# Splitting the early output weights into eight-partition DMAs in a DMA-bound decode kernel

## The chip, the cores and the metric

One core of one Trainium2 chip. The metric is the device time of one execution in microseconds (us); medians of several executions are quoted. One kernel's times agree within about 0.1 to 0.2% unless the text says otherwise.

## The reference

Eight sequences each decode one token: a layer norm with modulation, attention over a cache of 8192 keys and values with 8 key/value heads and 32 query heads, the output projection with `wo`, then a small MLP. Cut to what matters:

```python
# B = 8, D = 512, Hq = 32, Hkv = 8, Sk = 8192, Dh = 128, all bf16
h = layernorm(x) * (1 + ca) + sa
q = (h @ wq)                                   # 8 x 32 heads x 128
scores = einsum('bhqd,bhkd->bhqk', q, k_cache) * Dh ** -0.5
p = softmax(scores)
o = einsum('bhqk,bhkd->bhqd', p, v_cache)
x = x + ga * (o.reshape(B, 1, Hq * Dh) @ wo)   # wo: 4096 x 512
...                                            # layer norm, modulation
x = x + gb * (relu(h @ w1 + b1) ** 2 @ w2 + b2)
```

The two caches are 268 MB of the 284 MB that the kernel moves. `wo` is 4 MB.

## The kernel before

The caches come as 64 units of 4 MB, 128 rows (SBUF partitions) by 32 KB, through a ring of four slots. SyncE (SP) issues all of these DMAs in order on one queue. A unit's slot is loaded again as soon as TensorE has read it.

```python
units = [(kv, b, p) for b in range(B) for kv in "kv" for p in range(NP)]   # NP = 4
...
def load(n):
    kv, b, p = units[n]
    s = n % NSLOT
    src = ...                                    # 128 partitions x 32 KB
    dep = [released.get(s)]
    if units[n] == last:
        ...                                      # the last V unit, in four pieces
    else:
        loaded[n] = dma("sync", s_ring[s], lambda e: e.dma_start(slot(s), src), dep)
...
load(0)
load(1)
d_b1 = ...; d_b2 = ...                           # two small rows
wo_e = wo_sb[:, 0:24, :].rearrange("p (g j) n -> p g (j n)", j=4)
d_woe = dma("sync", s_woe, lambda e: e.dma_start(       # the early output weights, 3 MB
    wo_e, A_wo[0:24 * DH, :].rearrange("(g p j) n -> p g (j n)", g=6, p=128)))
d_wo = dma("sync", s_wo, lambda e: e.dma_start(         # the late output weights, 1 MB in 1 KB runs
    wo_sb[:, 24:32, :], A_wo[24 * DH:, :].rearrange("(h dh) n -> dh h n", dh=DH)))
load(2)
load(3)
```

TensorE transposes each K unit, computes scores with it, later multiplies the V units, and at the end runs the output projection and the MLP. The end needs, in this order, the last two V units, then W1 and W2, which lie in ring slots and are loaded last. The early output weights are used only at the end, so it doesn't matter when they land; what matters is whose time they take.

## Time and profile before

The kernel took 680.5 us (680.34 to 680.65).

| what | before | where it is read |
|---|---|---|
| span of the profiled execution | 677.9 us | the page |
| DMA share, rate in the middle | above 90%, 430 GB/s | the page's slices |
| TensorE busy | 73% | the page |
| K unit 2 (the first loaded behind the output weights) lands | 59.86 to 61.64 us | completion semaphores in the trace |
| unit due at 634 us lands | 623.20 to 627.32 us on eight engines, 632.46 to 634.31 us on the other eight | the same |
| last V piece lands | 652.5 to 656.7 us on eight, 661.9 to 663.74 us on eight | the same |
| last W2 piece lands | 664.3 to 665.7 us on eight, 672.2 to 673.95 us on eight | the same |

How to read it: in the trace the completion semaphore of every DMA of 128 rows climbs in 16 steps, one from each DMA engine when its own part has landed, and so these steps show how far apart the engines are. "Lands on eight at ..." means eight of these steps.

From the page of the kernel before: the span, the DMA lines of the slices (40 equal slices; busy share in tenths, then GB/s), the instruction queue (packets, MB, share of the 16 engines' span), and the chain that ended last, by engine.

```profile
span 677.9 us, 15869 instructions
...
DMA  8999999999999999999999999999999999999994
GB/s 365 439 400 434 430 431 433 430 431 425 424 433 429 428 431 433 432 430 431 432 433 425 418 432 430 429 427 431 431 433 432 430 424 426 431 429 431 427 393 160
...
q8 instruction: 57, 0.93, 0.6%
...
PE 49%; DMA 45%; DVE 3%; ACT 2%; issue 1%; SPq 0%
```

The DMA engines are the bound: they are above 90% from the second slice to the last but one. The chain is TensorE for half of it, because each batch has a stretch in which TensorE works on units that have already landed; but each such stretch begins when a landing lets it. Queue 8 is the engines' own instruction fetch: 57 packets of 16 KB (the Trainium skill, "Runtime: NRT & Kernel Launch", "Instruction fetch mechanics", gives blocks of 16 KiB, 256 instructions; 57 packets carry 0.93 MB here, which agrees). Each takes about 1.07 us. The trace doesn't name the engine of a packet. That they go in turn to only eight of the 16 DMA engines is read from the landings: eight engines fall behind, one of them at each fetch. Seven fetches of 1.07 us are 7.5 us, most of the distance between the two groups in the table, but not all: after 48 fetches, six for each of the eight, the medians of the two groups are already 9.3 us apart (the unit that lands from 584.4 to 594.0 us), or about 1.5 us for each fetch. The engines that fall behind keep the lag from unit to unit, and the kernel ends with them.

The chain of waits of the kernel before at both ends of the run, in order of time (start us, us, what).

```profile
23.18 38.46 DMA ring<-in_A_k_cache_dram
61.64 0.05 issue
61.69 3.60 PE PS L344 x32
```

```profile
569.44 24.57 DMA ring<-in_A_k_cache_dram
594.06 6.41 PE PS L344 x64
...
648.68 25.27 DMA ring<-in_B_w_dram
674.00 0.82 PE PS L569 x24
```

TensorE starts K unit 2 when it lands (61.69 us), starts the last batch when its first K unit lands (594.06 us), and waits once more for W2 (674.00 us). The waits of the kernel before after 600 us (engine, line, what it waited for: us in total, times, longest) show how little slack there is at the end:

```profile
PE PS L438 <- DMA ring<-in_A_v_cache_dram: 0.9, 1, 0.9
...
PE PS L569 <- DMA ring<-in_B_w_dram: 0.2, 1, 0.2
```

Two short waits: anything that delays the latest engine by more than a microsecond delays the end by nearly as much, and anything that makes it earlier gains about one microsecond.

The last view is SP's own timeline in the kernel before: start, duration, line, operation. Where a DMA instruction is long, many packets were still waiting in front of it: that of K unit 2 ended at 44.91 us.

```profile
3.46 0.40 SPq L323 DMA_DIRECT2D wo_sb<-in_A_wo_dram  x1
3.90 19.24 SPq L325 DMA_DIRECT2D wo_sb<-in_A_wo_dram  x1
23.18 22.60 SPq L261 DMA_DIRECT2D ring<-in_A_k_cache_dram  x2
```

### The profile page before, as it was taken

The numbers are of one execution on the slowest core, as the hardware profiler recorded it, in microseconds if no ns is written. First come the engines' busy times: TensorE is split into PE (matmuls) and PEld (weight loads), VectorE is DVE, ScalarE is ACT, GpSimd is POOL, SyncE is SP. The second block draws the span as 40 slices with busy tenths as digits, with TensorE's granted clock in tenths as the row PEclk, the third lists the DMA queues.
The fourth block names the chain that finished last, engine by engine and source line by source line (L and its number), as shares of the span: only waits on it lengthen the run. The fifth ranks groups of instructions, "written<-read, shape, count | busy, mean of one in ns | idle before, by whom it ended". The sixth has DMA issues, their size and how long they took to land.

```text
span 677.9 us, 15869 instructions
## 1 busy us (share of the span) xinstructions
PE 496.7 (73%) x7372; PEld 352.5 (52%) x7372; DVE 298.4 (44%) x558; ACT 234.9 (35%) x280; POOL 16.7 (2%) x66
## 2 busy tenths in 40 slices
PE   2394964997649965698548975499656987399777
PEld 2383731775237741576317752387325763187535
DVE  2062731567116751367215661167513673156712
ACT  2052620465006630265204650056302652046600
POOL 7200000000000000000000000000000000000000
PEclk9996985899769977799868987599766997589975
DMA  8999999999999999999999999999999999999994
GB/s 365 439 400 434 430 431 433 430 431 425 424 433 429 428 431 433 432 430 431 432 433 425 418 432 430 429 427 431 431 433 432 430 424 426 431 429 431 427 393 160
DMA packets 13733, 284.67 MB, mean 420 GB/s; under 512 B 1218, under 2 KB 2275, under 8 KB 4708
## 3 DMA queue, kind: packets, MB, share of 16 engines
q1 hardware_dynamic: 13620, 283.65, 98.0%
q8 instruction: 57, 0.93, 0.6%
q14 instruction: 8, 0.07, 0.0%
q10 hardware_dynamic: 48, 0.02, 0.0%
HBM read 283.66 MB, written 0.01 MB: 418 GB/s over the span
## 4 chain that ended last, share of the span: by engine, by line
PE 49%; DMA 45%; DVE 3%; ACT 2%; issue 1%; SPq 0%
DMA ring<-in_A_k_cache_dram 37%; PE PS L344 33%; PE PS L359 8%; DMA ring<-in_A_v_cache_dram 4%; DMA ring<-in_B_w_dram 4%; PE PS L438 3%; PE PS L401 3%; ACT KTb L349 1%; ACT P_sb L392 1%; DVE m L364 1%; PE PS L419 1%; DVE Pm L414 0%; DVE rinv L420 0%; DVE rhs_r L417 0%; DVE Dm L385 0%
## 5 line engine op out<-in xcount | busy, mean ns | idle before, releaser
L349 ACT ACTIVATE KTb<-PS 128x1024 bf16<-128x1024 bf16 x192 | 196.5, 1024 | 378.3 <-PE PS L344 378.3
L344 PE MATMUL PS<-IDENT,ring 128*128 128x128 bf16 x4096 | 269.6, 229 | 46.3 <-DMA ring<-in_A_k_cache_dram 46.2
L344 PEld LDWEIGHTS PS<-IDENT,ring 128*128 128x128 bf16 x4096 | 248.9, 103 | 95.1 <-DMA ring<-in_A_k_cache_dram 48.8
L351 DVE COPY KTb<-PS 128x1024 bf16<-128x1024 bf16 x320 | 210.2, 687 | 149.7 <-PE PS L344 147.6
L438 PE MATMUL PS<-ring,Pm 128*32 128x512 bf16 x992 | 87.7, 516 | 50.2 <-DMA ring<-in_A_v_cache_dram 45.9
L359 PE MATMUL PS<-KTb,QTm 128*32 128x512 bf16 x1024 | 79.2, 386 | 4.5 <-ACT KTb L349 4.5
L447 DVE CAST O_sb<-PS 128x512 bf16<-128x512 f32 x31 | 21.4, 692 | 130.4 <-PE PS L438 130.4
L438 PEld LDWEIGHTS PS<-ring,Pm 128*32 128x32 bf16 x992 | 30.8, 120 | 88.3 <-DMA ring<-in_A_v_cache_dram 47.1
L450 PE MATMUL PS<-SEL,O_sb 128*128 128x8 bf16 x124 | 22.5, 181 | 30.4 <-DVE O_sb L447 24.8
L450 PEld LDWEIGHTS PS<-SEL,O_sb 128*128 128x128 bf16 x124 | 12.0, 97 | 59.4 <-DVE O_sb L447 45.9
L401 PE MATMUL PS<-IDENT,P_sb 128*64 128x128 bf16 x512 | 26.1, 278 | 10.3 <-ACT P_sb L392 10.0
L401 PEld LDWEIGHTS PS<-IDENT,P_sb 128*64 128x64 bf16 x512 | 22.2, 146 | 13.0 <-ACT P_sb L392 12.6
L392 ACT ACTIVATE P_sb<-PS,negm 128x512 bf16<-128x512 f32 x32 | 21.5, 685 | 18.9 <-DVE negm L389 18.9
L414 DVE COPY Pm<-PS 64x512 bf16<-64x512 bf16 x48 | 20.2, 421 | 16.8 <-PE PS L401 15.8
L359 PEld LDWEIGHTS PS<-KTb,QTm 128*32 128x32 bf16 x1024 | 15.5, 94 | 21.1 <-ACT KTb L349 8.5
L364 DVE TENSOR_REDUCE m<-PS 128x1 f32<-128x512 f32 x32 | 22.0, 689 | 6.6 <-PE PS L359 6.6
L453 DVE TENSOR_TENSOR oTn<-PS,rinv 128x8 bf16<-128x8 f32 x31 | 6.0, 194 | 31.1 <-PE PS L450 31.1
L411 ACT ACTIVATE Pm<-PS 64x512 bf16<-64x512 bf16 x16 | 9.5, 592 | 6.4 <-PE PS L401 6.4
L304 PE MATMUL PS<-haT,ring 128*128 128x8 bf16 x128 | 3.6, 168 | 8.2 <-DMA ring<-in_A_wq_dram 8.2
L419 PE MATMUL PS<-rhs_r,ONES 128*128 128x32 f32 x16 | 4.4, 365 | 6.8 <-DVE rhs_r L417 6.8
L549 ACT ACTIVATE std<-PS,epst 128x8 f32<-128x8 f32 x1 | 0.3, 267 | 26.0 <-PE PS L547 26.0
L387 PE MATMUL PS<-Dm,R 128*128 128x4 bf16 x8 | 1.4, 178 | 10.1 <-DVE Dm L385 10.1
(110 smaller groups left out, 94.9 us busy)
## 6 DMA issues: line engine op xcount, KB each, us to landing
ring<-in_A_k_cache_dram SPq DMA_DIRECT2D x32, 4096.0 KB, 34.8
ring<-in_A_v_cache_dram SPq DMA_DIRECT2D x31, 4096.0 KB, 29.2
ring<-in_A_wq_dram SPq DMA_DIRECT2D x1, 4096.0 KB, 20.5
ring<-in_w_mod_dram SPq DMA_DIRECT2D x1, 3072.0 KB, 9.8
wo_sb<-in_A_wo_dram SPq DMA_DIRECT2D x1, 3072.0 KB, 45.5
ring<-in_A_v_cache_dram SPq DMA_DIRECT2D x1, 2048.0 KB, 24.0
ring<-in_B_w_dram SPq DMA_DIRECT2D x1, 1792.0 KB, 20.4
wo_sb<-in_A_wo_dram SPq DMA_DIRECT2D x1, 1024.0 KB, 48.0
```

The source lines that it names most:

```text
L344: t = op("tensor", lambda e, j=j, i=i: e.matmul(STG[j][:, i, :], src[:, 32 * k + 8 * j + i, :], IDENT[:, :], is_transpose=True), [loaded[n ...
L349: stg_free[j] = op("scalar", lambda e, j=j, dst=dst: e.activation(dst, STG[j], ACT.Copy), [t])
L351: stg_free[j] = op("vector", lambda e, j=j, dst=dst: e.tensor_copy(dst, STG[j]), [t])
L359: t = op("tensor", lambda e, hf=hf, q=q, rhs=rhs: e.matmul(PS[32 * q:32 * (q + 1), k, :], QTm[:, b, 2 * p + hf, :], rhs, start=(p == 0 and ...
L364: return op("vector", lambda e: e.tensor_reduce(m4[:, k:k + 1], bank(k), AX.X, ALU.max), [t])
L392: exps.append(op("scalar", lambda e, k=k: e.activation(P_sb[:, k, :], bank(k), ACT.Exp, bias=negm[:, 0:1], scale=inv_sqrt, accum_out=rs4[: ...
L401: t = op("tensor", lambda e, k=k, i=i, hf=hf, src=src: e.matmul(STG[k][64 * hf:64 * (hf + 1), i, :], src, IDENT[:, :], is_transpose=True, ...
L414: done.append(op("vector", lambda e, dst=dst, frm=frm: e.tensor_copy(dst, frm), [t, k_pm]))
L419: t = op("tensor", lambda e: e.matmul(tot_ps, ONES[:, :], rhs_r[:]), [t])
L438: t = op("tensor", lambda e, p=p, m=m, cg=cg, vt=vt, Obank=Obank: e.matmul(Obank[32 * cg:32 * (cg + 1), :], lhs[:, p, 32 * m:32 * m + 32], ...
L447: t = op("vector", lambda e, osb=osb, Obank=Obank: e.tensor_copy(osb, Obank), [t])
L450: t = op("tensor", lambda e, i=i, osb=osb, oT_ps=oT_ps: e.matmul(oT_ps, osb[:, i * 128:(i + 1) * 128], SEL[:, i, :], start=(i == 0), stop= ...
```

## The change

The early output weights are 128 rows of six 4 KB packets, 48 packets on each engine. The change splits them into twelve DMAs, of which ten have eight rows, one has 16 and one 32. The intent: a DMA of eight rows uses only the first eight DMA engines. So these carry 78 of the packets each, and the other eight carry 18. At some 0.16 us for a packet (0.159 to 0.164 in the trace), 30 packets, 4.9 us of work, move from one half of the engines to the other. If the half that gets less is the half that runs late, the end comes sooner.

```diff
+        wo_er = A_wo[0:24 * DH, :].rearrange("(g p j) n -> p g (j n)", g=6, p=128)
+
+        def wo_part(sl):
+            return dma("sync", s_woe, lambda e: e.dma_start(wo_e[sl], wo_er[sl]))
+
+        for r in range(3):
+            for blk in range(4 if r < 2 else 2):
+                wo_part(slice(32 * blk + r, 32 * blk + r + 29, 4))
+        wo_part(slice(64 + 2, 64 + 2 + 61, 4))
+        d_woe = wo_part(slice(3, 128, 4))
-        d_woe = dma("sync", s_woe, lambda e: e.dma_start(
-            wo_e, A_wo[0:24 * DH, :].rearrange("(g p j) n -> p g (j n)", g=6, p=128)))
```

The slices with stride 4 are chosen so that a piece on partitions 0 to 63 writes one row through each of eight SBUF ports. The Trainium skill, "DMA: Bandwidth & Descriptors", "The descriptor swizzle", says which engine writes which partitions in a 128-row DMA: engines 0 to 7 write partitions 0 to 63, and engines 8 to 15 write 64 to 127. By that map the pieces on partitions 64 to 127 make the first eight engines write through ports that the other eight otherwise have to themselves. From here on, "lower" means the first eight engines, "upper" the other eight, "own-port pieces" those on partitions 0 to 63, and "other-port pieces" those on 64 to 127.

SP's list of DMAs grows by eleven; no other engine's instructions change their order.

## The prediction

> **What bounds the kernel.** The DMA engines. In the windows from 100 to 600 us the DMA share is 1.00 at about 430 GB/s; TensorE is busy 73%. The chain of waits is 45% DMA, 49% TensorE: each batch's TensorE work starts when its first K unit lands (594.06 us for the last).
>
> The 16 DMA engines don't finish together. Completion semaphores in the trace: all 16 parts of K unit 1 land within 1.80 us (by 41.27 us); the unit due at 634 us lands at 623.20 to 627.32 us on eight engines, at 632.46 to 634.31 on eight; the last W2 piece at 664.3 to 665.7 and 672.2 to 673.95. The difference is instruction traffic: 57 packets of 16 KB on the instruction queue, about 1.07 us each, in turn over eight engines: 7 x 1.07 = 7.5 us each. Followed packet by packet, the first three fetches (16.1, 28.2, 43.0 us) fell on engines that carried nothing of the eight-row loads of c and x. The Trainium skill, "DMA: Bandwidth & Descriptors", "Why a DMA increments its semaphore by 16 and not by 1": a DMA of 8 rows uses the lowest-numbered eight engines. So I take the late ones to be the upper eight.
>
> **What the change does.** The same 768 packets of 4 KB (0.16 us each): before 48 per engine, after 78 on each lower, 18 on each upper. 30 x 0.16 = 4.9 us moves from the late to the early half. Eleven more issues on SP (0.2 to 0.5 us each) cost nothing.
>
> **What it could give.** Both halves would end near 669 us. The last V units would land up to 2.4 us earlier, but TensorE's end chain waits only 0.9 us for V (653.78) and 0.2 us for W2 (674.0): 1 to 2 us.
>
> **Why I doubt it.** DMAs are issued in order, and a full queue on one engine stops the issue to all. Before shows it: the issue of the late output weights lasts 19.2 us, that of K unit 2 21.7 us (to 44.91, with some 80 descriptors per engine outstanding); the last W2 piece is issued at 660.6 us although the early engines had run dry at 659.3. After, the lower queues hold 78 packets, then 65 entries of late weights. K unit 2 gets through when about 80 remain there, an estimate of 49 to 50 us; the upper engines, starved from 42 us, start K unit 2 then, against 49.8 before. The 4.9 us become idle time, except that three engines make up one fetch.
>
> Besides, pieces on partitions 64 to 127 and stride-4 pieces share SBUF write ports ("SBUF — State Buffer", "Door 1: The DMA port swizzle"); no trace of before shows such sharing. Estimate: 0 to 3 us longer on the lower engines, holding the upper too.
>
> **Predicted:** 680.8 us, range 678.4 to 684.0; faster by over 2% 0.01, within 2% 0.98, slower by over 2% 0.01.
>
> **Right if:** DMA share dips between 42 and 50 us; the issue of K unit 2 ends at 48 us or later; it lands on the upper engines no earlier than 59.9 us, on the lower at 64 to 68; TensorE starts it after 64 us (61.69 before); the last W2 piece lands within 3 us of 673.95.
>
> **Wrong if:** issue isn't held by the full lower queues (upper landings 4 to 5 us earlier, time 678 to 679), or the late engines are the lower eight (683 to 686).

## The result, and the profile after

688.02 us (687.79 to 688.87, four executions), against 680.45 (680.34 to 680.65, four) before. The ratio is 1.0113, with a 95% interval of 1.0096 to 1.0131. Ratios here are the mean time of one kernel's fast runs over that of the other's of the same rounds, so they are not quite the ratios of the medians quoted beside them. The change is slower by 7.6 us, which is within the 2% band, but far outside the predicted range of 678.4 to 684.0. The profiled execution was the slowest of the four (688.87), so the differences between the two traces come out about 1 us larger than 7.6.

From the page of the kernel after, the same lines (its instruction queue has one packet more, 58):

```profile
span 686.8 us, 15880 instructions
...
DMA  8999999999999999999999999999999999999992
GB/s 368 441 284 403 434 427 430 427 428 431 428 436 430 427 427 430 432 426 431 428 432 427 430 431 428 433 428 429 428 428 430 428 432 430 436 426 428 426 375 107
...
q8 instruction: 58, 0.95, 0.6%
...
PE 52%; DMA 42%; DVE 4%; ACT 2%; issue 1%; SPq 0%
```

The loss is visible in a single slice: the third (34 to 51 us), where the output weights are loaded, moved 284 GB/s instead of 400, though the engines were just as busy by the record. Busy engines that move less have slower packets. That stretch in windows, first before, then after (from:to, length, the busy time of each compute engine, TensorE clock, then the two columns to look at: DMA share and GB/s):

```profile
core 0: us, PE busy (x) PEld busy (x) DVE busy (x) ACT busy (x) POOL busy (x), PEclk, DMA share, GB/s
39.00:42.00 3.00, 3.00 (x54) 2.47 (x52) 2.10 (x4) 1.81 (x2) 0.00 (x0) 1.00 0.94 380
42.00:45.00 3.00, 3.00 (x54) 2.37 (x55) 2.09 (x4) 2.16 (x3) 0.00 (x0) 1.00 1.02 406
45.00:48.00 3.00, 3.00 (x50) 2.05 (x46) 2.13 (x4) 1.71 (x3) 0.00 (x0) 1.00 1.03 392
48.00:51.00 3.00, 3.00 (x53) 2.47 (x52) 1.98 (x3) 1.51 (x3) 0.00 (x0) 1.00 1.16 407
```

```profile
39.00:42.00 3.00, 3.00 (x55) 2.37 (x56) 2.12 (x4) 1.78 (x2) 0.00 (x0) 1.00 0.91 291
42.00:45.00 3.00, 3.00 (x50) 2.05 (x50) 2.10 (x4) 2.05 (x2) 0.00 (x0) 1.00 1.00 218
45.00:48.00 3.00, 3.00 (x55) 2.47 (x52) 1.64 (x3) 2.05 (x2) 0.00 (x0) 1.00 1.08 284
48.00:51.00 3.00, 3.00 (x54) 2.47 (x51) 2.05 (x4) 1.54 (x2) 0.00 (x0) 1.00 0.78 185
```

Packet by packet, the trace of after shows two different things in these windows:

- Packets of the own-port pieces take 0.159 to 0.164 us, as before. Those of the other-port pieces take 0.30 to 0.32 us between 42 and 45 us, when upper engines work too (on what they have of the output weights), and 0.28 to 0.30 us between 47 and 50 us. The upper engines pay too: their 1 KB packets of the late output weights take 0.08 to 0.10 us beside them, 0.047 to 0.051 before.
- From 48 to 51 us the DMA share falls to 0.78: from about 49.5 us upper engines have nothing to do, because K unit 2 hasn't been issued to them yet. From 50 to 52 us only about 8.2 packets are under way at a time.

SP's timeline in the kernel after:

```profile
3.56 35.19 SPq L327 DMA_DIRECT2D wo_sb<-in_A_wo_dram  x12
38.79 1.02 SPq L334 DMA_DIRECT2D wo_sb<-in_A_wo_dram  x1
39.87 13.09 SPq L261 DMA_DIRECT2D ring<-in_A_k_cache_dram  x2
```

The x2 on the last line are K units 2 and 3; the issue of unit 2 alone lasts from 39.87 to 52.14 us. So upper engines start K unit 2 at 52.85 to 53.0 us, about 3 us later than before (49.6 to 50.1 on most engines), although they have 30 packets fewer in front of it.

| lands (us) | before | after |
|---|---|---|
| K unit 2, upper eight | 59.9 to 61.6 (all 16) | 63.58 to 64.52 |
| K unit 2, lower eight | | 68.09 to 70.28 |
| last V piece, the two latest engines | 663.63, 663.74 | 670.96, 672.21 |
| last V piece, the other late engines | 661.9 to 663.5 | 665.6 to 667.1 |
| last W2 piece, the two latest engines | up to 673.95 | 679.81, 681.03 |

The sum: lower engines land K unit 2 about 8.1 us later. That is 4.9 us for 30 more packets and 3.2 us more for slow ones (the 24 packets of the four other-port pieces at about 0.30 us in place of 0.16 make some 3.3 us). Upper engines land it about 3.5 us later, in place of 4.9 us sooner. By the times above, as an estimate, slow packets took about 4.5 us of this gain (the engines run dry at 49.5 us, and finished at 49.9 before), waiting for the issue took 3.4 us, and a slow first packet of K unit 2 took 0.8 us (2.07 us, 1.28 before). From there on the engines stream without a pause, and the shift stays to the end. The chain of the kernel after, in order of time, at the same two places:

```profile
39.87 30.41 DMA ring<-in_A_k_cache_dram
70.28 0.05 issue
70.33 3.23 PE PS L353 x32
```

```profile
575.05 27.37 DMA ring<-in_A_k_cache_dram
602.42 0.05 issue
602.47 5.17 PE PS L353 x64
...
632.06 30.23 DMA ring<-in_A_v_cache_dram
662.34 3.63 PE PS L447 x32
```

TensorE starts K unit 2 8.6 us later (70.33 against 61.69), the last batch 8.4 us later (602.47 against 594.06), and the last V unit but one 8.6 us later (662.34 against 653.78). Of the waits of the kernel after, past 600 us, that for V grew from 0.9 to 3.1 us. The 4.4 us for K is not new: it is the start of the last batch, which in the kernel before ended a wait as long at 594.06 us, outside this window.

```profile
PE PS L353 <- DMA ring<-in_A_k_cache_dram: 5.1, 2, 4.4
...
PE PS L447 <- DMA ring<-in_A_v_cache_dram: 3.1, 1, 3.1
```

### The profile page after: what moved, and what is told of

Same layout as the page of the kernel before. It is cut to its first block, busy times and chain, and to the rows that moved or that the text cites. A ratio compares the mean times of both kernels' runs of the same rounds, so it can differ in the third digit from the quotient of the medians.

```text
span 686.8 us, 15880 instructions
## 1 busy us (share of the span) xinstructions
PE 495.5 (72%) x7372; PEld 349.8 (51%) x7372; DVE 298.2 (43%) x558; ACT 235.0 (34%) x280; POOL 16.8 (2%) x66
## 4 chain that ended last, share of the span: by engine, by line
PE 52%; DMA 42%; DVE 4%; ACT 2%; issue 1%; SPq 0%
DMA ring<-in_A_k_cache_dram 37%; PE PS L353 33%; PE PS L368 8%; DMA ring<-in_A_v_cache_dram 4%; PE PS L447 4%; PE PS L410 3%; ACT KTb L358 1%; ACT P_sb L401 1%; DVE Pm L423 1%; DVE m L373 1%; PE PS L428 1%; PE PS L517 0%; PE PS L501 0%; DVE rinv L429 0%; PE PS L459 0%
## 5 line engine op out<-in xcount | busy, mean ns | idle before, releaser
L353 PE MATMUL PS<-IDENT,ring 128*128 128x128 bf16 x4096 | 266.8, 227 | 56.4 <-DMA ring<-in_A_k_cache_dram 56.4
L353 PEld LDWEIGHTS PS<-IDENT,ring 128*128 128x128 bf16 x4096 | 246.3, 102 | 104.9 <-DMA ring<-in_A_k_cache_dram 60.3
L447 PE MATMUL PS<-ring,Pm 128*32 128x512 bf16 x992 | 90.4, 529 | 50.3 <-DMA ring<-in_A_v_cache_dram 46.0
L447 PEld LDWEIGHTS PS<-ring,Pm 128*32 128x32 bf16 x992 | 31.1, 122 | 89.7 <-DMA ring<-in_A_v_cache_dram 47.1
L462 DVE TENSOR_TENSOR oTn<-PS,rinv 128x8 bf16<-128x8 f32 x31 | 6.0, 194 | 31.1 <-PE PS L459 31.1
```

Of the source, the lines that this page charges most:

```text
L353: t = op("tensor", lambda e, j=j, i=i: e.matmul(STG[j][:, i, :], src[:, 32 * k + 8 * j + i, :], IDENT[:, :], is_transpose=True), [loaded[n ...
L447: t = op("tensor", lambda e, p=p, m=m, cg=cg, vt=vt, Obank=Obank: e.matmul(Obank[32 * cg:32 * (cg + 1), :], lhs[:, p, 32 * m:32 * m + 32], ...
```

## The experiments

The theory after reading the result had two parts. **Who**: the late engines aren't just the upper eight; the change put work on an engine that was already the latest. **How**: writing partitions that belong to other engines' ports makes packets slow, on the writer and on those whose ports they are. Rivals: (A) the late engines are all of the lower eight, so the change moved work the wrong way for all; (B) eleven more DMAs cost something by themselves; (C) the stopped issue is the larger part (SP can't hand out K unit 2 to any engine while the queues of the lower ones are full); (D) the place in the queue is at fault, and pieces spread over the run would cost little. Fourteen kernels ran, some beside each other on the same chip. The expectations use the letters C and D a little differently, and say each time what they mean. In the short diffs "-" is the kernel that is named and "+" the experiment.

### m_before and m_after: who is late?

Tiny DMAs of 16, 8, 4, 2 and 1 rows ("markers") are issued behind the last W2 piece, the last load of all, and one of 8 rows directly behind the output weights. Each engine that takes part reports its arrival behind everything queued before on it. The Trainium skill, "DMA: Bandwidth & Descriptors", "Why a DMA increments its semaphore by 16 and not by 1", says that a DMA of k rows uses the lowest-numbered k engines. So an 8-row marker tells the lower eight apart from the rest, and a 4-row marker splits the lower eight.

```diff
+        def marker(i, rows, n):
+            return dma("sync", s_mk[i], lambda e: e.dma_start(mk_sb[0:rows, 176 * i:176 * i + n], w_mod[0:rows, 0:n]))
...
+        d_mk = [marker(5, 8, 144)]                 # behind the output weights
...
+                    d_mk += [marker(i, r, n) for i, (r, n) in enumerate(((16, 160), (8, 164), (4, 168), (2, 172), (1, 176)))]
```

> The kernel before with six tiny marker DMAs: one of 8 rows between the late output weights and K unit 2, and five of 16, 8, 4, 2 and 1 rows behind the last W2 piece. The packets of a marker of k rows show when each of the first k engines gets there. My theory (made after the result, from two late landings among the eight that got more work): the eight engines that carry instruction fetches are six of the upper eight and two of the lower eight. Then the 8-row marker at the end is reached by six engines at about 664 to 666 us and by two at about 672 to 674, and the 16-row one shows six more at 672 to 674. Rival A, late engines are the lower eight: all eight at 672 to 674. The premise of my prediction, late engines are the upper eight: all eight at 664 to 666. Time as before, 680 to 682 us.

> The changed kernel with the same markers. My theory: the middle 8-row marker is reached by the lower eight at about 57 to 60 us, so the engines whose K unit 2 lands at 63.6 to 64.5 are the upper eight, and those of 68.1 to 70.3 the lower eight; at the end the two lower engines with instruction fetches are the last of all (about 680 us), 8 to 9 us later than in the kernel before, the upper six 3 to 4 us later. Rival A: at the end all eight lower engines are last. Time about 688 us.

Measured: 680.24 and 688.25 us (one execution each, so their state is unknown; the kernel before gave 680.19 beside them, and 688.02 is the median of the kernel after), so the markers cost nothing that can be seen.

| marker at the end | in the kernel before | in the kernel after |
|---|---|---|
| 4 rows | 665.25 to 665.58, all early | 672.9 to 673.2 |
| 8 rows | six at 664.85 to 665.33, two at 671.97 and 672.13 | six at 672.5 to 673.0, two at 679.40 and 679.94, the last of all |
| 16 rows | eight at 664.54 to 665.30, eight at 671.85 to 673.76 | six more (the upper late ones) at 675.8 to 677.6 |

What follows: the eight engines with the instruction fetches are six of the upper eight and two of the lower eight. The 4-row marker is early on all, so the two are among the fifth to the eighth engine. Rival A falls, and so does the premise of the change and of the prediction. The change moved 4.9 us away from six late engines, and onto two late ones. In the kernel after the mid-run marker of 8 rows reached the lower engines at 57.65 to 59.37 us and they are the late group at K unit 2. The nesting of the results (all four early, six of eight early, eight of 16 early) agrees with the page's "lowest-numbered".

### x_extra8 and x_extra4: the bytes alone, on their own ports

The kernel before, plus one 2 KB packet on each of the first eight (or first four) engines at every unit from the fifth to the last but one, into unused memory on those engines' own ports. Over these 59 units that is about the 4.9 us of the change (at some 0.08 us a packet, half of a 4 KB one), spread out so that no queue fills.

```diff
+                if n >= 4:
+                    i = n % 8
+                    rows = slice(32 * (i % 2) + i // 2, 32 * (i % 2) + i // 2 + 29, 4)   # x_extra4: + 13
+                    idle[i] = dma("sync", s_idle[i], lambda e: e.dma_start(
+                        idle_sb[rows, :], A_wo[0:16, :].rearrange("(p j) n -> p (j n)", j=2)), [idle[i]])
```

> The kernel before, plus after each K or V load from unit 4 on a useless 8-row load of 2 KB rows (59 of them, about 0.08 us each) to rows whose ports belong to the lower eight engines anyway. So 4.8 us more work for each lower engine, without shared ports, without a full queue, and nothing taken from the upper ones. My theory (two of the lower eight are among the late engines): the last W2 piece lands about 4.8 us later, time 684 to 686. The premise of my prediction (the lower eight are early and have some 7 us of slack): within 1 us of before.

> The same useless loads with 4 rows, so that only the first four engines carry them: 4.8 us more on each of these. My theory (the markers put both late lower engines among the fifth to the eighth): within 1 us of before, as these four have 6 to 7 us of slack. Rival B (what costs is the number of DMAs, not who carries them): as slow as with 8 rows.

Measured: x_extra8 685.32 against 680.29 us (1.0074, 1.0059 to 1.0089); x_extra4 680.09 against 680.29 (0.9999, 0.9982 to 1.0016). In x_extra8 the last V piece lands on two engines at 668.85 and 668.88 us (663.6 and 663.7 before) and on the other late ones at 661.9 to 663.4, as before. So extra bytes on eight engines cost 5.0 us through two of them alone, and the same on the first four cost nothing. This is the bytes' share of the loss, and it shows that the slack at the end is below what was moved.

### x_twelve_even and x_rows32: more DMAs, but evenly spread

The early weights in twelve DMAs of 128 rows (half of a 4 KB run each), or in four DMAs of 32 rows with stride 4.

```diff
-        d_woe = dma(... wo_e, A_wo[0:24 * DH, :]...)          # x_twelve_even, from the kernel before
+        for g in range(6):
+            for h in range(2):
+                d_woe = dma("sync", s_woe, lambda e, g=g, h=h: e.dma_start(
+                    wo_e[:, g, 1024 * h:1024 * h + 1024], wo_er[:, g, 1024 * h:1024 * h + 1024]))
```
```diff
-        (the twelve pieces)                                   # x_rows32, from the kernel after
+        for r in range(4):
+            d_woe = wo_part(slice(r, 128, 4))
```

> The early output weights in twelve DMAs of 128 rows (one group of rows, half the columns each), so as many DMAs as the change has, but with equal shares of bytes on all engines. My theory (unequal shares, shared ports and stopped issue make the loss): within 1 us of before. Rival B (the number of DMAs on SP, and what each costs, makes the loss): 684 us or more.

> The same weights in four DMAs of 32 rows, stride 4, over all 128 partitions: equal bytes, and as the 32-row stage of the loading kernel ran at 0.16 us a packet, no shared ports. My theory: within 1 us of before. If the stride of 4 itself or small DMAs cost: like the 16-row pieces.

Measured: 680.57 against 680.19 us (1.0004, 0.9987 to 1.002) and 680.19 against 680.29 (1.0, 0.9985 to 1.0015). Rival B falls: twelve DMAs cost nothing that can be seen. x_rows32 also says what slow packets are not: a DMA of fewer rows with stride 4 over all partitions, which loads all ports evenly, runs at 0.159 us a packet.

### x_pairs16: the ports alone, with the engines evenly loaded

Eight DMAs of 16 rows, each within one half of the partitions. Every engine carries 48 packets, as before, but 16 engines write through eight ports at a time.

```diff
-        (the twelve pieces)                                   # from the kernel after
+        for h in range(2):
+            for r in range(4):
+                d_woe = wo_part(slice(64 * h + r, 64 * h + r + 61, 4))
```

> The early output weights in eight DMAs of 16 rows, stride 4, within one half of the partitions: equal bytes on every engine (48 packets each), but in each piece two engines write each port. My theory (shared ports cost): packets of 0.30 to 0.32 us in place of 0.16, K unit 2 lands about 7 us later on all engines, time 686 to 688. Rival C (only the unequal bytes and the stopped issue cost): within 1 us of before.

Measured: 688.32 against 680.29 us (1.012, 1.0105 to 1.0135), slightly above what was expected. Packets take 0.327 to 0.333 us, and K unit 2 lands at 67.81 to 70.06 us on all engines together. 48 x (0.33 - 0.16) = 8.2 us: port sharing costs as much as the whole change here, without any imbalance between engines.

### ports: the sharing by itself

A small kernel (97.39 us; its output is wrong, relative error 0.085) that loads pieces in stages, each waiting for the one before.

```python
stage("a128", A(0, 128))                       # 128 rows
stage("b8even", A(0, 29, 4))                   # 8 rows on the lower engines' ports
stage("c8odd", A(64, 93, 4))                   # 8 rows on the upper engines' ports, those at rest
stage("d8four", A(0, 8))                       # 8 rows on two ports
stage("e16even", A(0, 61, 4))                  # 16 rows within 0..63
stage("f16odd", A(66, 127, 4))                 # the change's 16-row piece
stage("g32", A(3, 128, 4))                     # the change's 32-row piece
stage("h64", A(0, 64))                         # 64 rows
stage("i_even_kv", ..., kvload=True)           # four own-port pieces, then a K unit
stage("j_odd_kv", ..., kvload=True)            # four other-port pieces, then a K unit
stage("k_kv", kvload=True)                     # a K unit alone
```

> The disputed cost by itself: a kernel that only loads, one stage after the other, 4 KB rows of the output weights and 32 KB rows of K; its output is wrong on purpose. If engines that write partitions of the same SBUF port share its rate: 128 rows 0.16 us a packet; 8 rows at stride 4 on partitions 0 to 28 or, alone, on 64 to 92 0.16 us; 8 rows on partitions 0 to 7 (two ports, four engines each) about 0.6 us; 16 rows at stride 4 within 64 partitions and 64 rows 0..63 about 0.30 us; four 8-row pieces of partitions 0 to 63 followed by a K unit: no stretching; four of partitions 64 to 127 followed by a K unit: 0.30 us for these and 2.1 to 2.4 us for the upper engines' 32 KB packets that run at the same time. If it is not the ports (but, say, the short DMAs themselves): the odd and the even pieces behave alike, and the 16-row piece takes 0.16 us a packet.

| stage | 4 KB packet | rate over the whole stage |
|---|---|---|
| 128 rows | 0.159 us | 366 GB/s |
| 8 rows, own ports | 0.159 us | |
| 8 rows, other ports, those engines at rest | 0.159 us | |
| 8 rows on two ports | 0.61 to 0.63 us at its end | 84 GB/s |
| 16 rows within one half (both stages) | 0.159 us for about 1.2 us, then 0.31 to 0.33 us | 167 to 178 GB/s |
| 32 rows, stride 4 | 0.159 us | |
| 64 rows | 0.319 us | 219 GB/s |

A packet is slow when its port serves two engines at once, and not when the port is merely another engine's. The Trainium skill, "SBUF — State Buffer", "Door 1: The DMA port swizzle", gives eight ports for partitions 0 to 63, and an asymptote of about 218 GB/s for them. The run is near it: 219 GB/s over the whole stage, its faster start included, and 205 GB/s in the steady part (16 packets of 4 KB in 0.319 us). With a K unit behind, the four other-port pieces land within 4.7 us of the first, the own-port pieces within 3.3 us. But a K unit alone also began with packets of 1.5 to 2.1 us, so these stages couldn't say what other-port pieces do to a full stream. That took ports2, below.

### x_before_tail and x_after_tail: is the stopped issue the larger part?

The late output weights (64 packets of 1 KB on each engine, in front of K unit 2) are moved behind the ninth unit, in the kernel before and in the kernel after. K unit 2 is then issued with little in front. (x_moved, below, ran before these two; it is "the last run" of the second expectation.)

```diff
             ...
+            if n == 8:
+                d_wo.append(dma("sync", s_wo, lambda e: e.dma_start(
+                    wo_sb[:, 24:32, :], A_wo[24 * DH:, :].rearrange("(h dh) n -> dh h n", dh=DH))))
...
-        d_wo = dma("sync", s_wo, ...)                          # from behind the early weights
```

> The same move of the late output weights alone, in the kernel before. All partitions, equal bytes, own ports: within 1 us of before.

> The changed kernel with the late output weights (65 entries in each engine's queue) moved behind unit 8, so that only the twelve pieces stand before K unit 2. If the number of entries in the lower queues is what stops the issue, the issue of K unit 2 ends before 46 us (52.1 in the changed kernel) and the upper engines start it by then instead of at 52.7. Since the last run showed that pieces to the other half's ports stretch 32 KB packets on all engines, I expect that this earlier start buys little or nothing: 686 to 692 us. If the stopped issue were the larger part of the loss: 684 or less.

Measured: 680.27 against 680.21 us (1.0, 0.9986 to 1.0015) and 691.02 against 680.21 (1.0157, 1.014 to 1.0174). SP's timeline in x_after_tail:

```profile
3.51 35.35 SPq L331 DMA_DIRECT2D wo_sb<-in_A_wo_dram  x12
38.90 2.11 SPq L262 DMA_DIRECT2D ring<-in_A_k_cache_dram  x2
```

K unit 2 is issued by 39.9 us instead of 52.14, and upper engines begin it at about 45 us, earlier than before the change. The windows of x_after_tail (columns as above):

```profile
45.00:48.00 3.00, 3.00 (x53) 2.10 (x50) 2.30 (x4) 1.72 (x3) 0.00 (x0) 1.00 1.09 328
48.00:51.00 3.00, 3.00 (x55) 2.31 (x48) 2.10 (x4) 1.77 (x2) 0.00 (x0) 1.00 1.12 246
51.00:54.00 3.00, 2.11 (x36) 1.51 (x33) 1.29 (x3) 2.05 (x2) 0.00 (x0) 1.00 0.95 257
```

The dip in the DMA share is gone (1.12 where after had 0.78), but the rate is only 246 to 257 GB/s: the K packets of 32 KB, 1.21 us elsewhere, now take 1.5 to 2.4 us beside the other-port pieces. The kernel is slower by 3 us than the change. Rival C falls: the stopped issue is real, but it kept upper engines from a collision that costs more.

### x_moved: the same pieces, one per unit, in the full stream

```diff
+            if 8 <= n < 8 + 12:
+                d_wo_e.append(wo_part(pieces[n - 8]))
...
-        (the twelve pieces behind load(1))                     # from the kernel after
+        pieces = [...]                                         # the same slices, as a list
```

> The twelve pieces of the change, the same partitions and engines, but issued one by one behind the K and V units 8 to 19, so that the lower queues never fill and the issue isn't stopped. My theory, from the terms measured so far: the upper engines are no longer held (K unit 2 lands near 60 us on all, as before), but the two late lower engines keep the 30 packets (4.9 us) and their shared ports (3 to 5 us, as the pieces for partitions 64 to 127 now meet the upper engines' K and V packets), so time 685 to 690, the two latest landings of the last V piece at 671 to 674. Rival D (the stopped issue makes most of the loss): 682 or less.

Measured: 696.11 against 680.07 us (1.0231, 1.0218 to 1.0244), 16 us slower; my range was missed by 6 us, and rival D by far. Own-port pieces leave the packets beside them as they are (4 KB 0.161 us, 32 KB 1.22 us). Other-port pieces take 0.26 to 0.29 us a packet, and while one is under way the 32 KB packets of **all** engines stretch to 1.7 to 2.3 us, together 27 to 33 us too long for one piece, or about 2 us on each of 16 engines. The landings say the same: even the least delayed engine falls back by 1.6 to 2.3 us with each of these pieces, though a piece has only six packets (1.0 us) for an engine that carries it. The last V piece lands on the two latest engines at 679.5 and 679.7 us (16 us later than before), and on the others of the late group at about 668 to 670.6 us, six to seven us later. I had counted the sharing only on the ports concerned.

### x_four and x_four_here: can the two late engines be spared?

If the two late lower engines were all of the cause, burdening only the first four engines, which are early, would be harmless. Both kernels load three quarters of the weights in 32-row pieces and the rest in eight pieces of four rows: the first four engines carry 84 packets (36 of the 48 extra ones through other engines' ports), the other twelve 36. x_four spreads the eight pieces over units; x_four_here keeps them where the change has its own.

```diff
-        (the twelve pieces)                                    # from the kernel after
+        for q in range(8):                                     # in x_four: one behind each of the units 8 to 15
+            wo_part(slice(3 + 16 * q, 3 + 16 * q + 13, 4))
+        for r in range(3):
+            d_woe = wo_part(slice(r, 128, 4))
```

> A version that takes bytes from all late engines: 96 rows in three 32-row pieces at the start, the other 32 rows in eight 4-row pieces behind units 8 to 15, so the first four engines (none late) carry 84 packets and the other twelve 36 in place of 48. If engines are the limit: the late landings come 12 x 0.16 = 1.9 us earlier, time 678 to 679. If the SBUF port is the limit[...]: the rows still go to the late engines' ports, each foreign packet takes its time from them, and the late landings move by less than 0.7 us, time within 0.6 us of before. I expect the second.

> At the place of the change: eight 4-row pieces (84 packets in all on each of the first four engines, 36 on the other twelve), then three 32-row pieces, then the late weights and K unit 2. The full queues of the first four engines stop the issue as in the change, but no late engine gets more work. My theory: K unit 2 reaches the others 3 to 4 us later than before, the first four have enough slack, so the loss is that of the held engines alone: 682.5 to 685.5 us. If the place and the stopped issue alone make the change's loss, with whom it burdens of no account: 687 to 689 us.

Measured: x_four 687.09 against 680.07 us (1.0093, 1.0071 to 1.0115), and unusually scattered (683.82 to 688.39 in six executions). Neither theory expected a loss; both missed. With fewer packets in front of it, K unit 2 landed 1.7 to 2.1 us earlier than before on all engines. As soon as the first other-port pieces came, all 16 landings moved back by 1.3 us or more, and after all six of them (36 packets on each carrier, 5.8 us) no engine was less than 4.4 us behind the kernel before. x_four_here: 686.79 against 680.3 us (1.0101, 1.0084 to 1.0118), between what the two theories expected (682.5 to 685.5, and 687 to 689). The issue of K unit 2 ends at 54.8 us; twelve engines land it at 66.1 to 66.75 us, about 6.2 us later than before, and four at 70.4 to 71.2.

So sparing the two late engines saves only about 1 us of 7.6. But x_four_here isn't the change with these two spared and nothing else: it has more other-port packets per carrier (36 against 30) and holds the issue longer. Its twelve engines run dry at about 53.2 us, where they finished at 49.9 us before, although they have 1.9 us less to do: slow packets took some 5 us. Then they wait another 2.4 us for the issue and start K unit 2 at 55.5 to 55.9 us. Both other-port writes and the stopped issue delay the engines that were to be relieved; the run doesn't separate what each does to the total.

### ports2: what an other-port piece does to everybody

A small kernel again (207.52 us, wrong output): each stage issues a K unit, two pieces, and two more K units at once, and waits for all. The pieces are 12 packets on each engine that carries them, 12 x 0.16 = 1.9 us.

```python
stage("a_none")
stage("b_own8", A(0, 29, 4), A(32, 61, 4))        # lower engines, own ports
stage("c_other8", A(64, 93, 4), A(96, 125, 4))    # lower engines, ports of the upper ones
stage("d_own4", A(0, 13, 4), A(32, 45, 4))        # engines 1 to 4, own ports
stage("e_other4", A(16, 29, 4), A(48, 61, 4))     # engines 1 to 4, ports of 5 to 8
stage("f_again")
```

> A kernel that only loads (its output is the input x, wrong on purpose): six stages of a K unit, two pieces of 4 KB rows, and two more K units. Own ports: the piece's engines end 12 x 0.16 = 1.9 us late, the others not at all. If only engines that share a port delay each other: with 4-row pieces to the ports of the fifth to eighth engine, eight engines are late and eight end as in the stage without pieces. If something wider is shared: all sixteen end late. I expect the second, as all sixteen landings moved by at least 1.3 us in the run with 4-row pieces spread out.

Landing of the third K unit, in us from the stage's first issue:

| stage | engines without pieces | engines with pieces |
|---|---|---|
| none (first and last) | 31.1 to 31.5, 31.0 to 31.9 | |
| own ports, 8 | eight at 31.1 to 31.6 | eight at 33.0 to 33.45 (+1.9) |
| other ports, 8 | eight at 33.1 to 33.7 (+2.0) | eight at 34.8 to 35.7 (+3.9) |
| own ports, 4 | twelve at 31.0 to 31.7 | four at 33.0 to 33.4 (+1.9) |
| other ports, 4 | twelve at 32.9 to 33.5 (+1.9) | four at 35.0 to 35.4 (+3.9) |

On own ports only the engine that carries a packet pays for it. With other ports, every engine is delayed by the time of the twelve packets that one carrier has, whether four or eight engines carry, and the carriers by that once more. In x_moved the delay for the same number of packets was about twice as long, so this is no fixed price. In the last row pieces go through the ports of four engines, and yet twelve are delayed, eight of which neither carry pieces nor own the ports. Ports that are shared don't explain these eight; something wider than a port is held up. What it is stays open: the trace shows only that their packets take longer.

## Why the prediction was wrong

- **Bound and lateness: right.** The DMA engines bound the kernel, eight run late, one more at each instruction fetch, and the end follows the latest. Only the size, "7.5 us each", was too small: 9.3 us after six rounds of fetches.
- **"So I take the late ones to be the upper eight": wrong.** This is the step that failed. The markers show six of the upper eight and two of the lower eight. The inference came from three fetches that fell on engines without rows of the small loads; three out of eight engines don't identify the group. With x_extra8 the bytes alone, through the two, cost 5.0 us. The prediction took the late group to have 4.9 us less to do; its latest two members in the kernel after had got 4.9 us more. An estimate of what this step did: the landings of the other six at the last V piece moved by only about 3 us (mean 666.3 against 663.3 us for the late eight before), so with these alone the end would have come some 2 to 3 us later, inside the range.
- **"Estimate: 0 to 3 us longer on the lower engines, holding the upper too": too small, and of too narrow a kind.** On the lower engines it was 3.2 us, just above the range. But it came on top of an increase, not of a decrease, and upper engines were held by it: they land K unit 2 3.5 us later where they should have gained. x_pairs16 shows sharing alone worth 8 us, and ports2 that twelve other-port packets on each carrier, 1.9 us, put all 16 engines 1.9 us or more behind in a full stream.
- **Stopped issue: right, but for its length.** The issue of K unit 2 ended at 52.14 us (predicted 48 or later), the DMA share fell to 0.78 in the window from 48 to 51 us, upper engines landed K unit 2 at 63.6 us or later (predicted not before 59.9), and TensorE started it at 70.33 us (predicted after 64). But "starved from 42 us" and "the 4.9 us become idle time" were wrong: upper engines worked until about 49.5 us, as slow packets had taken some 4.5 us of their gain, and then waited 3.4 us. And it isn't where the time went: x_after_tail took it away and lost 3 us more.
- **Lower engines land K unit 2 "at 64 to 68": wrong**, 68.09 to 70.28 us. **Last W2 piece "within 3 us of 673.95": wrong**, 681.03.
- **More issues cost nothing: right** (x_twelve_even, x_rows32).
- **The listed exceptions.** "The late engines are the lower eight (683 to 686)" was the nearest, but neither cause nor size was that: a quarter of the late group was enough, and 688.0 also contains the sharing.

The account of the 7.6 us: the latest engines are two of the lower eight. They have 4.9 us more bytes and 3.2 us of slower packets, 8.1 us in all. By the markers at the end they are 7.4 and 7.8 us later. In the profiled execution, which was 1 us slower than the typical one, the two latest landings of the last V piece come 7.3 and 8.5 us later, and the end, with about a microsecond of slack, follows. The six late engines that were to be relieved are later too, by about 3 us at the last V piece. The 3.2 us are read from the trace of after; x_extra8 and x_pairs16 show that extra bytes and shared ports each cost time alone, and no run takes only the sharing out of the change.

Why nothing was to be had even with the right engines, as far as the runs show: to move a row from one engine to another is to write it through a port that isn't the new engine's own, since the row's partition doesn't change. By ports2 this delays all 16 engines, in a full stream, by about the time of the packets that one carrier has. So an engine that is relieved of 30 packets gains 4.9 us and, by that measure, loses about as much. In x_four the twelve engines that were relieved of 12 packets each were about 2 us early at first, and more than 4 us late once the six other-port pieces had passed. Of the twelve kernels that compute the whole result none was faster than the one before.

## What to carry to other kernels

To relieve a DMA engine by giving fewer rows to it, first find out by markers which engines are late (a DMA of 8, 4, 2 rows reports the lowest-numbered ones), as an inference from a few packets can mistake the two engines that decide. Then look where the rows go in SBUF: here a piece whose ports were in use by other engines had packets at half speed and, beside a full stream, held up every engine. Even splits cost nothing that could be seen, neither twelve DMAs of 128 rows nor four of 32 rows with stride 4.

## What the Trainium skill lacked or had wrong

- "Runtime: NRT & Kernel Launch", "Instruction fetch mechanics", calls the cost of a fetch mostly hidden. For a DMA-bound kernel it isn't: eight particular DMA engines, six of the upper eight and two of the fifth to eighth, fall behind one by one as 57 packets of 16 KB (about 1.07 us each) pass, by 9.3 us after 48 of them, and the kernel ends with them. No page says which engines carry fetches.
- "SBUF — State Buffer", "Door 1: The DMA port swizzle", explains a shared port (205 GB/s in the steady part for 64 rows, 219 over the whole stage, near its 218). It doesn't say that writes through other engines' ports, beside a full stream, delay all 16 engines: +1.9 us on twelve engines for 1.9 us of packets on four, and +3.9 us on these four. The nearest that the pages have, the back-pressure in "DMA: Bandwidth & Descriptors", is about transfers between cores.
- The same section gives no sign that a short piece escapes: sixteen rows on eight ports ran at 0.159 us a packet for about 1.2 us before they fell to 0.31 to 0.33 us. (The page's next section has small transfers miss the port's rate too, but because of their fixed cost.)
- "DMA: Bandwidth & Descriptors", "Queues, rings and completion order", doesn't say that a queue that is full on some engines stops the issue to all: the issue of one K unit lasted 12.27 us in the kernel after (21.73 us before), and upper engines were dry for 3.4 us meanwhile.
- "DMA: Bandwidth & Descriptors", "Why a DMA increments its semaphore by 16 and not by 1": nothing wrong; nested markers of 4, 8 and 16 rows agree with "the lowest-numbered k" (4 early of 4, 6 of 8, 8 of 16); of these the page lists only 16 as seen.
